# The convolution half of a fused block: from an order written out by hand to tasks of the list scheduler

## The chip, the cores and the metric

The kernel runs on one core of one Trainium2 chip. The metric is the device time of one execution in microseconds (us). A core has five engines with an instruction stream each: PE (matrix multiply, with PEld for its weight loads), DVE (vector), ACT (scalar activation), POOL and SP. Each engine executes its stream in program order and waits on semaphores where an operand is not there yet. In this kernel SP issues nearly all DMA transfers, so SP's order is the order in which transfers are asked for.

## The reference, cut to what matters

```python
def _A_ref(q, k, v, shift_k, ssm_k, ssm_D):       # S = 2048, D = 512, ks = 4
    k_shift = sum(k_pad[:, t:t + S, :] * shift_k[:, ks - 1 - t] for t in range(ks))
    kv = k_shift * v
    y = irfft(rfft(kv, 2 * S) * rfft(ssm_k, 2 * S))[:S]     # causal convolution along S
    y = y + kv * ssm_D
    return q * y
def _B_ref(x, w1, w2, w3, w4):                    # F = 1792
    h = gelu(layernorm(x) @ w1)
    x1 = x + shifted_by_channel_quarter(h) @ w2
    return x1 + gelu(layernorm(x1) @ w3) @ w4
h = x + _A_ref(layernorm(x), A_k, A_v, ...)       # x = A_q
out = h + _B_ref(layernorm(h), ...)
```

Inputs and output are bf16 of shape (1, 2048, 512); sums are in float32.

## The kernel before, in words

The kernel has two halves. The **first half** (lines 218 to 499) computes the convolution `_A_ref` with a Fourier transform of length 4096 in two steps, both as matmuls. The **second half** (lines 501 to 770) does the inverse's last step, the gate with q, and all of `_B_ref`.

The first half goes through these stages; the names are those of the functions and of the tiles in the profile.

- **Loads.** SP issues the filter `A_ssm_k` in 4 pieces into `ra` (L229), k in 4 transposing transfers into `rb` (L232), v in 2 into `rb` (L236). q comes later (L374).
- **Tables.** DVE and ACT compute sines for the transform (`trig`, L321 to L330, table `ftab` in `rf`) from angles that DVE forms at L315 and L318.
- **Transposed filter** (L356 to L361). PE turns the filter in 8 blocks of 8 transposes, ACT empties five of them and DVE three. L364 adds the D row.
- **First step of the filter** (`step1`, L348, 16 times): 8 matmuls into a double bank `ps`, 128x1024 float32, that DVE or ACT evicts into `rc`. After each 4 of them an **exchange** (L353) of 4 transfers moves the result across partitions into `rd`, 16 in all.
- **Shift and product** (`shift`, L406 and L409, 16 times): 16 matmuls with diagonal weights make the four-tap shift of k, DVE multiplies by v into `xk`.
- **First step of k*v** (`step1` again, 16 times, into `ra`) and its exchange into `rc` (L353).
- **Second step of the filter** (`spectrum`, L396, tile `psg`, 16 times): 4 matmuls, evicted into `rd`.
- **Transposed tables** (`tables`, 4 times) and the inverse's table (`backs`).
- **Statistics of q** (`qstat`, L414 and L415, 16 times, on DVE), closed by `qnorm` on POOL.
- **The loop of products** (L493 to L496, 16 turns): `fwd` does the second step of k*v (`psk`), ACT spreads it to `asb` (L339), DVE makes two products with the filter's spectrum (`pr`, L473 and L474); two turns later `inv` does 8 matmuls (L484) into `psv` or `psva`, evicted into `vst`, and SP sends it across partitions into `ra` (L488).

The order of all that is the order of the Python code. One loop (from L433 on) puts a shift, a first step of k*v, a spectrum and a statistic of q behind each other in every turn; the rest of the spectra and the tables follow it, and the loop of products comes last. `evac` (L335) sends an eviction to ACT or DVE by a running count of their costs. PSUM has three double banks (`ps_a`) for most stages and two single ones (`ps_c`) for shifts, transposes and tables; the loop of products gives those two to `psv`. `xk` has 8 buffers, `asb`, `pr` and `vst` have tiles of their own.

The second half is ordered by the class `Plan` (L35). Each task has a cost for each engine that may do it, a list of tasks that it depends on, and rings of buffers that it takes and drops. `forward` is a list scheduler that gives each free engine the ready task of highest priority; `solve` repeats it 40 times with other priorities and keeps the shortest plan; `emit` writes the instructions in that order. The costs set only the order: on the chip every engine runs its stream as soon as its operands are there. The second half's first task is `inv1` (L549), then the gate (`z`, L560, on ACT).

Of the kernel before, what the change touches and what calls it, by code (L numbers as in the profile page):

```python
# [34 lines left out]
class Plan:  # L35
# [6 lines left out]

    LAT = 0.2

    def __init__(self, pools, rounds=40):
        self.pools, self.rounds, self.t = pools, rounds, []

    def add(self, opts, fn, deps=(), take=None, many=1, drop=None, part=0, rank=0.0, name=None):
        n = len(self.t)
        deps = {d["n"] for d in deps if d is not None}  # L50
        if drop is not None:
# [3 lines left out]
                 users=[0] * many, rank=rank, name=name)  # L55
# [5 lines left out]
    def forward(self, prio):  # L61
        ts = self.t
        done, eng, free, order = {}, {}, {e: 0.0 for t in ts for e in t["opts"]}, []
# [4 lines left out]
        while ready:  # L68
            best = None
            for n in ready:  # L70
# [7 lines left out]
                at0 = {e: max([at0, free[e]] + [done[d] + (0.0 if eng[d] == e else self.LAT) for d in t["deps"]]) for e in t["opts"]}  # L78
# [12 lines left out]
            if t["drop"] is not None:  # L91
                m, i = t["drop"]
                users[m][i] -= 1
                if not users[m][i]:
                    gone[m, i] = done[n]
# [6 lines left out]
        return max(done.values()), order, done, eng  # L102

    def backward(self, done, eng):
# [4 lines left out]
        while ready:  # L109
            best = None  # L110
            for n in ready:
                e = eng[n]
                at = max([free[e]] + [left[o] + (0.0 if eng[o] == e else self.LAT) for o in ts[n]["out"]])
# [12 lines left out]
    def solve(self):  # L126
        tail, best, rnd = {}, None, random.Random(1)
        for t in reversed(self.t):
            tail[t["n"]] = t["rank"] + min(t["opts"].values()) + max((tail[o] + self.LAT for o in t["out"]), default=0.0)
# [18 lines left out]
def kernel(  # L148
# [69 lines left out]
    ps_a = p0.enter_context(tc.tile_pool(name="ps_a", bufs=3, space=PSUM))  # L218
    p1 = ExitStack()
    ps_c = p1.enter_context(tc.tile_pool(name="ps_c", bufs=2, space=PSUM))  # L220
    xkp = p1.enter_context(tc.tile_pool(name="xkp", bufs=8))
# [6 lines left out]
    for c in range(DC):  # L228
        nc.sync.dma_start(hnat[:, c, :], A_ssm_k[c * P:(c + 1) * P, :])  # L229
    k_r = A_k.rearrange("o n d -> (o n) d")  # L230
    for c in range(DC):
        nc.sync.dma_start_transpose(kT[:, c, 16:KW], k_r[:, c * P:(c + 1) * P])  # L232
    v_r = A_v.rearrange("o (p b) d -> p (o b) d", p=P)
    q_r = A_q.rearrange("o (p b) d -> p (o b) d", p=P)
    for g in range(2):
        nc.sync.dma_start(v_sb[:, 8 * g:8 * g + 8, :], v_r[:, 8 * g:8 * g + 8, :])  # L236
# [27 lines left out]
    for i in range(10):  # L264
        pt = ps_c.tile([P, D], F32, name="ptw", tag="pk")
        nc.tensor.matmul(pt[:], lhsT=wup[:, 0:P], rhs=wup[:], start=True, stop=True)
# [47 lines left out]
    for r in range(2):  # L314
        nc.vector.tensor_tensor(out=uu[:, :, r, :, :],  # L315
                                in0=a1[:].rearrange("p (k t) -> p k t", t=2).unsqueeze(3).to_broadcast([P, NH, 2, 32]),
                                in1=b2[:, r, :].unsqueeze(1).unsqueeze(1).to_broadcast([P, NH, 2, 32]), op=ADD)
    nc.vector.tensor_scalar(out=ui, in0=ui, scalar1=4095, scalar2=None, op0=OP.bitwise_and)  # L318

    def trig():  # L320
        nc.scalar.activation(fall[:, :, 0:32], uall, ACT.Sin, bias=negpi[:], scale=SC)  # L321
        nc.vector.tensor_scalar(out=fall[:, :, 32:64], in0=fall[:, :, 0:32], scalar1=sgo[:], scalar2=None, op0=MUL)
        nc.gpsimd.tensor_scalar(out=ftab[:, 0, :, 0, 0:32], in0=s0[:, :, 0, :], scalar1=lo_, scalar2=1.0, op0=MUL, op1=MUL)
# [8 lines left out]
    load = {"A": 0.0, "V": 0.0}  # L332

    def evac(o, i, n, fast=False, eng=None):
        ca, cv = 0.05 + 0.833e-3 * n, 0.065 + (0.52e-3 if fast else 1.042e-3) * n  # L335
        e = eng or ("A" if load["A"] + ca <= load["V"] + cv else "V")
        if e == "A":
            load["A"] += ca
# [28 lines left out]
    for bl in range(NL):  # L367
# [3 lines left out]
        if bl == 1:  # L371
            trig()
# [59 lines left out]
    for b in range(NB):  # L432
# [11 lines left out]
        if b >= 4:  # L444
            qstat(b - 4)
# [351 lines left out]
```

## Time and profile before

| | |
|---|---|
| median of 3 runs | 265.88 us (265.42 to 269.07) |
| the profiled execution's own time | 268.6 us |
| its span, first to last instruction | 266.8 us |
| mean granted clock of PE | 0.953 |
| busy: PE, DVE, ACT, POOL | 231.9, 161.9, 143.3, 54.1 us |
| moved by DMA | 28.08 MB |

The times are those of whole executions; the profile is one execution, 1.8 us of which lie outside the span. Its time is 2.7 us above the median. In a row of a group, the last number before the second bar is the mean duration in ns, and what follows it is how long the engine stood idle just before, and who ended that. A row of the chain of waits has start, length, engine, tile and line. PE's busy time counts matmuls that overlap, so a busy PE is not yet a full one.

### The profile page before, as it was taken

How to read it: one execution, taken by the hardware profiler on the slowest of the kernel's cores; microseconds unless marked ns; L12 is line 12 of the kernel's file. 1: busy time of each engine (PE TensorE's matmuls, PEld its weight loads, DVE VectorE, ACT ScalarE, POOL GpSimd, SP SyncE). 2: the span in 40 equal slices, each digit the busy share in tenths (PEclk: the TensorE clock that was granted, in tenths of full speed). 3: DMA queues.
4: the chain of work that ended last, by engine and by line, in shares of the span. 5: the costliest groups of instructions: out<-in, count | busy, mean ns of one | idle time of the engine just before them, and what ended most of it. 6: DMA issues, size and time to landing. Idle time of an engine off the chain costs nothing.

```text
span 266.8 us, 4530 instructions
## 1 busy us (share of the span) xinstructions
PE 231.9 (87%) x1803; PEld 119.0 (45%) x1803; DVE 161.9 (61%) x323; ACT 143.3 (54%) x202; POOL 54.1 (20%) x101
## 2 busy tenths in 40 slices
PE   8665957999579988665988999999999999999994
PEld 3522834555242222224655756445444444444441
DVE  7986807669927998299999994898022250013322
ACT  3638152788479998266867856556500046632000
POOL 3503000000130102029998442251000000000000
PEclk9999995999959999796899999999999999999999
DMA  7999990340701465891000000000011110000111
GB/s 241 249 271 360 407 346 37 142 160 15 295 11 41 153 241 179 295 396 39 1 2 0 4 0 0 2 1 0 2 39 39 39 39 2 0 20 20 42 39 39
DMA packets 18791, 28.08 MB, mean 105 GB/s; under 512 B 10065, under 2 KB 13906, under 8 KB 17234
## 3 DMA queue, kind: packets, MB, share of 16 engines
q1 hardware_dynamic: 17952, 26.74, 29.0%
q0 software_dynamic: 288, 1.05, 1.3%
q8 instruction: 14, 0.23, 0.4%
q10 hardware_dynamic: 530, 0.01, 0.1%
q14 instruction: 7, 0.06, 0.1%
HBM read 11.02 MB, written 2.10 MB: 49 GB/s over the span
## 4 chain that ended last, share of the span: by engine, by line
PE 57%; DVE 24%; DMA 6%; ACT 5%; POOL 4%; issue 2%; ACTq 0%; POOLq 0%
PE mm L717 18%; PE mm L702 18%; DVE st L566 4%; PE pk L406 4%; PE mm L662 3%; DVE rd L571 3%; DMA q_sb<-in_A_q_dram 3%; DMA rd<-rc 2%; DVE rt L315 2%; PE psg L396 2%; DVE vst L342 2%; ACT rc L339 2%; PE psk L396 2%; PE psva L484 2%; DVE pr L474 1%
## 5 line engine op out<-in xcount | busy, mean ns | idle before, releaser
L708 ACT ACTIVATE ra<-mm 128x512 bf16<-128x512 f32 x56 | 33.4, 597 | 49.7 <-PE mm L702 49.6
L702 PE MATMUL mm<-rc,rb 128*128 128x512 bf16 x224 | 50.8, 379 | 0.0
L717 PE MATMUL mm<-rt,ra 128*128 128x512 bf16 x224 | 49.0, 379 | 0.0
L725 DVE TENSOR_TENSOR ob<-mm,rd 128x512 bf16<-128x512 f32 x16 | 11.1, 692 | 61.4 <-PE mm L717 61.4
L717 PEld LDWEIGHTS <-ra 128*128 128x128 bf16 x224 | 22.0, 98 | 26.4
L702 PEld LDWEIGHTS <-rb 128*128 128x128 bf16 x224 | 21.6, 98 | 24.8
L406 PE MATMUL pk<-diag,rb 128*128 128x128 bf16 x256 | 19.8, 238 | 4.4 <-DVE xk L409 4.3
L406 PEld LDWEIGHTS <-rb 128*128 128x128 bf16 x256 | 18.3, 150 | 8.8 <-issue 7.5
L637 PE MATMUL mm<-rc,rf 128*128 128x256 bf16 x128 | 17.8, 295 | 0.0
L530 ACT COPY rc<-ptx 128x512 bf16<-128x512 bf16 x26 | 14.6, 583 | 4.6 <-PE ptx L623 4.6
L662 PE MATMUL mm<-rf,rb 128*128 128x512 bf16 x64 | 16.2, 380 | 1.0 <-ACT rb L643 0.9
L339 ACT CAST asb<-psk 128x1024 bf16<-128x1024 f32 x16 | 16.1, 1030 | 0.5 <-ACT asb L339 0.4
L571 DVE SCALAR_TENSOR_TENSOR rd<-q_sb,qmv,z 128x512 bf16<-128x512 bf16 x16 | 12.7, 792 | 4.6 <-ACT z L560 4.6
L414 DVE BATCH_NORM_STATS2 qst<-q_sb 128x6 f32<-128x512 bf16 x16 | 10.9, 680 | 6.5 <-DMA q_sb<-in_A_q_dram 6.5
L409 DVE TENSOR_TENSOR xk<-pk,rb 128x512 bf16<-128x512 f32 x16 | 10.9, 681 | 6.3 <-PE pk L406 6.2
L560 ACT ACTIVATE z<-mm,qrs 128x512 f32<-128x512 f32 x16 | 10.6, 697 | 7.4 <-PE mm L549 5.7
L637 PEld LDWEIGHTS <-rf 128*128 128x128 bf16 x128 | 13.2, 106 | 2.3
L667 DVE SCALAR_TENSOR_TENSOR q_sb<-rd,cr,mm 128x512 bf16<-128x512 bf16 x16 | 11.7, 733 | 3.7 <-PE mm L662 3.7
L396 PE MATMUL psg<-rd,rf 128*64 128x512 bf16 x64 | 10.3, 418 | 4.2 <-ACT rd L339 4.0
L396 PEld LDWEIGHTS <-rf 128*64 128x64 bf16 x128 | 5.7, 115 | 17.2 <-issue 16.2
L473 DVE TENSOR_TENSOR pr<-asb,rd 128x1024 bf16<-128x1024 bf16 x16 | 11.0, 687 | 3.5 <-ACT asb L339 3.5
L339 ACT CAST rd<-psg 128x1024 bf16<-128x1024 f32 x13 | 13.0, 1028 | 0.0
(224 smaller groups left out, 347.2 us busy)
## 6 DMA issues: line engine op xcount, KB each, us to landing
rd<-rc SPq DMA_DIRECT2D x16, 256.0 KB, 6.0
rc<-ra SPq DMA_DIRECT2D x16, 256.0 KB, 2.4
ra<-vst SPq DMA_DIRECT2D x16, 256.0 KB, 2.4
ra<-in_A_ssm_k_dram SPq DMA_DIRECT2D x4, 512.0 KB, 5.1
rb<-in_A_v_dram SPq DMA_DIRECT2D x2, 1024.0 KB, 8.0
q_sb<-in_A_q_dram SPq DMA_DIRECT2D x2, 1024.0 KB, 8.3
out_dram<-ob SPq DMA_DIRECT2D x16, 128.0 KB, 1.8
rb<-in_B_w_dram SPq DMA_DIRECT2D x1, 1792.0 KB, 7.3
```

Source lines behind the costliest of these rows:

```text
L339: nc.scalar.copy(o, i)
L396: nc.tensor.matmul(ps[64 * t:64 * t + 64, r, :], lhsT=ftab[:, kh, r, t, :], rhs=z[:, kh, t, :], start=True, stop=True)
L406: nc.tensor.matmul(pk[:, c * P:(c + 1) * P], lhsT=kT[:, c, 16 + b - j:KW - 16 + b - j + 1:16], rhs=diag[:, c, j, :], start=(j == 0), stop= ...
L530: nc.scalar.copy(o, i)
L571: nc.vector.scalar_tensor_tensor(out=h_sb[:, b, :], in0=q_sb[:, b, :], scalar=qmv[:, b, 0:1], in1=tl["z", b][:], op0=SUB, op1=MUL)
L637: nc.tensor.matmul(pw_[:, j * 256:(j + 1) * 256], lhsT=w1_sb[:, k, m * P:(m + 1) * P], rhs=hnT[:, k, p * 256:(p + 1) * 256], start=(k == 0 ...
L662: nc.tensor.matmul(px[:], lhsT=shifted(m, b), rhs=w2_sb[:, m, :], start=(m == 0), stop=(m == DC - 1))
L667: nc.vector.scalar_tensor_tensor(out=x1[:, b, :], in0=hbm[:, b, :], scalar=tl["cr", b // 2][:, b % 2:b % 2 + 1], in1=tl["x", b][:], op0=MU ...
L702: nc.tensor.matmul(pg[:], lhsT=w3_sb[:, k, fc * P:(fc + 1) * P], rhs=lnT[:, k, g * 512:(g + 1) * 512], start=(k == 0), stop=(k == DC - 1))
L708: nc.scalar.activation(gbuf[:, g % 2, fc, :], tl["g", g, fc][:], ACT.Gelu_apprx_tanh)
L717: nc.tensor.matmul(po[:], lhsT=gbuf[:, g % 2, fc, i * P:(i + 1) * P], rhs=w4_sb[:, fc, :], start=(fc == 0), stop=(fc == FC - 1))
L725: nc.vector.tensor_tensor(out=ob[:], in0=tl["o", 4 * g + i][:], in1=xh1[:, b, :], op=ADD)
```

## The change

The first half's stages become tasks of a `Plan` too. What that does:

- **DMA as an engine "D".** Each load and each exchange is a task with a cost on D and a landing latency `lat` of 1.75 us that its users wait for in the plan. D is SP's queue. The order of the loads becomes filter, k, then q, v, q, v in halves; the exchanges come behind all four.
- **One PSUM ring.** `ps_a` has 4 double banks, taken by every stage in turn; `ps_c` and `ps_v` are gone. Shifts are done in pairs, so that a product of k and v is 128x1024, once for two blocks. `xk` has 4 buffers of four blocks' width.
- **Product buffers in dead memory.** `asb` (3), `pr` (4) and `vst` (5 buffers) lie in `rb`, where k and v were. The first spread depends on the last shift and the last product with v.
- **Order.** The scheduler interleaves. Of the filter's 16 first steps four come behind the first shifts, 11 of its 16 spectra come into the loop of products, the inverse's table near its end. Table copies go whole to one engine, here DVE.

The arithmetic stays, and the number of transfers. The second half's plan has the same tasks, and its rows stand in the same order on all five engines.

Three places in the order. **SP from its first load**, `ra` being the filter's place, `rb` that of k and v, `rd<-rc` the filter's exchange and `rc<-ra` that of k*v. Before:

```order
L229 DMA ra<-in_A_ssm_k_dram 128x2048 x4
L232 DMA_TRANSPOSE rb<-in_A_k_dram 128x2048 x4
L236 DMA rb<-in_A_v_dram 128x4096 x2
L353 DMA rd<-rc 32x4096 x16
L374 DMA q_sb<-in_A_q_dram 128x4096 x2
L353 DMA rc<-ra 32x4096 x16
L488 DMA ra<-vst 32x4x1024 x16
```

And of the change:

```order
L329 DMA ra<-in_A_ssm_k_dram 128x2048 x4
L329 DMA_TRANSPOSE rb<-in_A_k_dram 128x2048 x4
L329 DMA q_sb<-in_A_q_dram 128x4096
L329 DMA rb<-in_A_v_dram 128x4096
L329 DMA q_sb<-in_A_q_dram 128x4096
L329 DMA rb<-in_A_v_dram 128x4096
L401 DMA rd<-rc 32x4096 x16
L401 DMA rc<-ra 32x4096 x16
L546 DMA ra<-rb 32x4x1024 x16
```

q has moved ahead of the filter's exchange, its first half ahead of v.

**DVE around the first product of spectra** (`pr` before, `rb<-rb,rd` in the change; `rt` are the tables, `rd<-psg` and `rd<-pg` spectra of the filter, `qst` and `qmv` a statistic of q). Before:

```order
L383 TENSOR_SCALAR rt<-pt 128x512
L390 TENSOR_SCALAR rt<-pt 128x128
L342 CAST rd<-psg 128x1024
L383 TENSOR_SCALAR rt<-pt 128x512
L342 COPY rt<-pt 128x512
L473 TENSOR_TENSOR pr<-asb,rd 128x1024
L474 TENSOR_TENSOR pr<-asb,rd 128x1024
```

And of the change:

```order
L474 TENSOR_SCALAR rt<-tb 128x512
L323 CAST rd<-pg 128x1024
L500 BN_STATS qst<-q_sb 128x6
L501 BN_AGGR qmv<-qst 128x2
L323 CAST rd<-pg 128x1024
L531 TENSOR_TENSOR rb<-rb,rd 128x1024
L532 TENSOR_TENSOR rb<-rb,rd 128x1024
```

The products stand where two of DVE's spectra are done; before, all of them were.

**ACT from the last first step of k*v into the loop** (`ra<-pc` that step, `asb<-psk` before and `rb<-pw` now the spread, `vst` before and `rb<-pv` now the inverse). Before:

```order
L339 CAST ra<-ps_1055 128x1024
L339 COPY rt<-pt 128x512 x2
L339 CAST rd<-psg 128x1024 x3
L339 CAST f_71<-ptf 128x512 x2
L339 COPY rt<-pt 128x512
L339 CAST asb<-psk 128x1024 x3
L339 CAST vst<-psva 128x1024
L339 CAST asb<-psk 128x1024
```

And of the change:

```order
L321 CAST ra<-pc 128x1024 x7
L321 CAST rd<-pg 128x1024 x3
L321 CAST rb<-pw 128x1024 x3
L321 CAST rd<-pg 128x1024 x2
L321 CAST rb<-pw 128x1024
L321 CAST rb<-pv 128x1024 x2
L321 CAST rb<-pw 128x1024
L321 CAST rb<-pv 128x1024
```

Spectra stand between spreads and inverses now, and no table copy is left on ACT here.

The diff, cut to its core:

```diff
-    ps_a = p0.enter_context(tc.tile_pool(name="ps_a", bufs=3, space=PSUM))
-    p1 = ExitStack()
-    ps_c = p1.enter_context(tc.tile_pool(name="ps_c", bufs=2, space=PSUM))
-    xkp = p1.enter_context(tc.tile_pool(name="xkp", bufs=8))
+    ps_a = p0.enter_context(tc.tile_pool(name="ps_a", bufs=4, space=PSUM))
+    xkp = p0.enter_context(tc.tile_pool(name="xkp", bufs=4))
...
+    plan = Plan({"big": 4, "xk": 4, "asb": 3, "pr": 4, "vst": 5}, 40, {"V": 5.6, "A": 6.2, "G": 2.8, "PE": 5.5, "D": 1.8})
...
+    EV = {"A": 1.04, "V": 1.2}
+    LAND = 1.75
...
+    for g in range(2):
+        task(("v", g), {"D": 3.0}, load(v_sb[:, 8 * g:8 * g + 8, :], v_r[:, 8 * g:8 * g + 8, :]), lat=LAND)
+    for g in range(2):
+        task(("q", g), {"D": 3.0}, load(q_sb[:, 8 * g:8 * g + 8, :], q_r[:, 8 * g:8 * g + 8, :]), lat=LAND)
...
+    task(("uu",), {"V": 2.4}, angles)
...
+    for bl in range(NL):
+        for h in range(4):
+            task(("F", bl, h), {"PE": 0.56}, step1(("ph", bl, h), lambda bq, bl=bl: xh[:, 4 * bl + bq, :], h),
+                 [("TE", c, bl // 2) for c in range(DC)] + [("dr",)], take="big")
+            task(("FE", bl, h), EV, out1(("ph", bl, h), zch, bl, h), drop=("F", bl, h))
+        task(("FX", bl), {"D": 2.6}, exchange(zh, zch, bl, range(4)), [("FE", bl, h) for h in range(4)], lat=LAND)
...
+    for p in range(NB // 2):
+        task(("S", p), {"PE": 2.3}, shift(p), [("k", c) for c in range(DC)] + [("diag",)] + ([("S", p - 1)] if p else []), take="big")
+        task(("X", p), {"V": 1.25}, gated(p), [("v", p // 4)] + ([("X", p - 1)] if p % 2 else []), take=None if p % 2 else "xk",
+             drop=("S", p))
+    for bl in range(NL):
+        for h in range(4):
+            task(("K", bl, h), {"PE": 0.56}, step1(("pc", bl, h), lambda bq, bl=bl: tl["xk", bl][:, bq, :], h),
+                 [("X", 2 * bl + 1)], take="big", drop=("X", 2 * bl))
+            task(("KE", bl, h), EV, out1(("pc", bl, h), zck, bl, h),
+                 [("F", 3, 3)] if bl > 1 else [("T", c, 1) for c in range(DC)], drop=("K", bl, h))
+        for kl in range(4):
+            task(("KX", bl, kl), {"D": 0.66}, exchange(zk, zck, bl, [kl]), [("KE", bl, h) for h in range(4)] + [("FX", 3)], lat=LAND)
...
+    for kb in range(4):
+        task(("B", kb), {"PE": 0.6}, tables(kb), [("tg",)], take="big")
+        task(("BE", kb), {"A": 1.7, "V": 1.1}, tabled(kb), drop=("B", kb))
...
+    for b in range(NB):
+        task(("qs", b), {"V": 0.85}, qstat(b), [("q", b // 8)])
+    task(("qn",), {"G": 3.3}, qnorm, [("qs", b) for b in range(NB)])
+    for kh in range(NH):
+        task(("G", kh), {"PE": 0.56}, step2(("pg", kh), zh, kh), [("FX", bl) for bl in range(NL)] + [("tg",)], take="big")
+        task(("GE", kh), EV, lambda e, kh=kh: copy(e, gst[:, kh, :, :], tl["pg", kh][:]), drop=("G", kh))
+
+    asb = [view(rb, 1024 * i, 1024, "p (r d) -> p r d", r=2) for i in range(3)]
+    prb = [view(rb, 3072 + 2048 * i, 2048, "p (m r d) -> p m r d", m=2, r=2) for i in range(4)]
+    vsb = [view(rb, 11264 + 1024 * i, 1024, "p (t d) -> p t d", t=2) for i in range(5)]
...
+    for kh in range(NH):
+        task(("W", kh), {"PE": 0.56}, step2(("pw", kh), zk, kh), [("KX", bl, kh // 4) for bl in range(NL)] + [("BE", kb) for kb in range(4)] + [("be",)] +
+             ([("V", kh - 3)] if kh > 2 else []), take="big")
+        task(("A", kh), {"A": 1.04}, spread(kh), [("S", NB // 2 - 1), ("X", NB // 2 - 1)], take="asb", drop=("W", kh))
+        task(("P", kh), {"V": 1.38}, products(kh), [("GE", kh)], take="pr", drop=("A", kh))
+        task(("V", kh), {"PE": 1.0}, inverse(kh), [("BE", kh // 4), ("be",)], take="big", drop=("P", kh))
+        task(("VE", kh), EV, lambda e, kh=kh: copy(e, ring("vst", vsb, ("vst", kh)), tl["pv", kh][:]), take="vst", drop=("V", kh))
+        task(("VX", kh), {"D": 0.66}, back(kh), [("KX", NL - 1, 3)], drop=("VE", kh), lat=LAND)
+    plan.emit()
```

336 lines of the change are left out of this document (161 added, 175 removed).

## The prediction

> **What bounds the kernel now.** I read the stretches first: one row for each stage, with busy time of PE, PEld, DVE, ACT and POOL, granted clock, DMA share and GB/s.
>
> ```profile
> 0.00:26.50 26.50, 17.40 (x186) 9.37 (x187) 21.33 (x45) 14.19 (x16) 8.26 (x28) 1.00 0.99 278
> 26.50:40.00 13.50, 10.72 (x156) 8.20 (x156) 5.73 (x7) 5.45 (x6) 0.08 (x1) 1.00 0.96 381
> 40.00:79.60 39.60, 33.10 (x381) 19.22 (x382) 27.55 (x54) 26.61 (x32) 3.15 (x2) 0.85 0.28 111
> 79.60:109.10 29.50, 25.10 (x191) 7.61 (x188) 25.47 (x37) 26.86 (x30) 2.44 (x4) 0.96 0.47 166
> 109.10:266.80 157.70, 145.62 (x896) 74.58 (x896) 81.80 (x181) 70.19 (x120) 40.16 (x67) 0.97 0.12 40
> ```
>
> The last row is the second half, which the change leaves alone. In the four rows of the first half DVE is busy 80.1 of 109.1 us, ACT 73.1, PE 86.3 (the third row's mean clock of 0.85 is a full clock with stretches at half, below). No engine is full there except in the fourth row, where ACT and DVE both stand near 90%. So the first half is bound by order: who waits for whom, and each stage waits for the one ahead. The chain of waits says where:
>
> ```profile
> 26.56 6.07 DMA rd<-rc
> 32.65 7.34 DMA q_sb<-in_A_q_dram
> 40.01 0.70 DVE qst L414
> 41.55 1.86 PE pk L406 x16
> ...
> 73.94 2.75 ACT rd L339 x3
> ...
> 80.65 0.70 DVE pr L473
> ```
>
> The reader is to see two seams. From 26.6 to 40.0 the chain is DMA: q is issued on SP behind the 16 exchange transfers, and DVE, in program order, stands at the statistics of q with the k*v products behind it. From 72 to 80 the loop of products has not begun, because the last spectra and tables are still being emptied. The list of waits gives these seams their prices:
>
> ```profile
> DVE qst L414 <- DMA q_sb<-in_A_q_dram: 6.5, 1, 6.5
> PE pk L406 <- DVE xk L409: 4.3, 1, 4.3
> PE psg L396 <- ACT rd L339: 4.0, 1, 4.0
> ```
>
> **The change, part by part.** Landmarks of the timeline (start, length), then lengths of work that follows work without a gap, from the chain:
>
> ```profile
> 27.59 5.18 PE L406 MATMUL pk<-diag,rb 128*128 128x128 bf16 x80
> 79.60 2.85 ACT L339 CAST asb<-psk 128x1024 bf16<-128x1024 f32 x3
> 107.45 1.23 DVE L342 CAST vst<-psv 128x1024 bf16<-128x1024 f32 x1 [0.70 <-PE psv L484]
> 112.54 2.42 ACT L560 ACTIVATE z<-mm,qrs 128x512 f32<-128x512 f32 x4 [4.85 <-PE mm L549]
> ```
>
> ```profile
> 14.02 0.41 DVE ra L364
> 14.48 0.64 PE ps_281 L348 x8
> 15.14 2.37 DVE rc L342 x2
> ...
> 70.14 0.59 DVE qst L414
> 70.93 0.59 DVE qst L414
> ...
> 78.62 0.42 DVE rt L342
> ...
> 84.13 0.55 PE psk L396 x4
> 84.68 0.97 PE psva L484 x8
> ...
> 95.88 0.60 DVE pr L474
> ```
>
> That gives: a 128x1024 eviction of PSUM 1.19 us on DVE (2.37 over 2) and 0.92 on ACT (2.75 over 3); a statistic of q 0.79; a 128x512 copy of a table 0.42; a pair of products 1.20; a second step 0.55 and an inverse 0.97 on PE; 32 shift matmuls 2.07 (5.18 over 80, times 32).
>
> *Start to 22 us.* DVE now empties four of the eight transposed blocks instead of three and flips the table's signs ahead of its phase evictions. Both were there before, later or on ACT:
>
> ```profile
> L342 DVE COPY ra<-pt 128x1024 bf16<-128x1024 bf16 x3 | 2.0, 685 | 0.1
> L322 DVE TENSOR_SCALAR rf<-rf,sgo 128x2048 bf16<-128x2048 bf16 x1 | 0.8, 754 | 2.6 <-ACT rf L321 2.6
> ```
>
> So the first step of the filter can start 0.7 us later than at 14.48, and DVE begins its evictions at 14.43 + 0.69 + 0.75 = 15.9. Five take 5.9, to 21.8; ACT takes seven at 0.92. Twelve of 16 steps are then done and PE is free for the shifts at about 22.5, where before it began them at 27.59.
>
> *Loads.* SP now issues q, v, q, v in halves behind the transposes of k, and the exchanges come after.
>
> ```profile
> L236 SPq DMA_DIRECT2D rb<-in_A_v_dram x2: 420/523/626, 15.6 to 16.2; - x2
> DMA to landing us min/median/max: 6.4/8.0/9.5
> ```
>
> The halves of v landed at about 15.6 + 6.4 = 22.0 and 16.2 + 9.5 = 25.7, that is 3.7 us apart. The first places in the queue are now q's: I estimate q at 22.0, v at 25.7, q at 29.4, v at 33.1. DVE's four first statistics run from 22.0 to 25.2 and the first product of k and v at 25.7, so the 6.5 us wait for q is gone. What is late next is the second half of v. The fifth product wants it, and its shift is ready at 22.5 + 5 x 2.07 = 32.9, so PE covers it; without that cover each us of a later v is a us of the end. Seven shifts keep PE until 22.5 + 7 x 2.07 = 37.0, and DVE's seventh product ends at 38.2. The product over 1024 columns has no row before; two rows of half its size would be 1.36 (681 ns each alone), an eviction of that size 1.19; I take 1.19, as DVE is fed from PSUM in both, and 0.17 x 8 = 1.4 us goes to the range.
>
> *From 38.2 to the first spectral product.* DVE's order lists: 7 statistics (5.5), the last product of k and v (1.2), 5 evictions of first steps (6.0), 12 table copies (5.0) with a small one (0.2), 2 spectra (2.4). Sum 20.3, so 58.5. PE, ACT and the four double banks are looser there: PE has 19 first steps, one pair of shifts, tables and five spectra, some 18 us, and ACT 14 evictions, 13 us. On SP the filter's fourth exchange now waits for the last of these evictions of ACT's, at about 45, and behind it in that queue stand all 16 transfers of k*v. They need 0.6 us each on SP and 2.4 to land:
>
> ```profile
> L353 SPq DMA_DIRECT2D rc<-ra x16: 459/593/601, 45.5 to 71.7; - x16
> rc<-ra SPq DMA_DIRECT2D x16, 256.0 KB, 2.4
> ```
>
> The first group of them is ready at about 46, so little waits there, and the spectra start after 52. The last eviction for k*v comes at about 52.5 on this count; four transfers and the landing make 57, ahead of the first product. I add 1.0 us for handoffs through one ring: 59.5, against 80.65 before. These 21 us are not all gain, since 11 of 16 spectra, before finished by then, now run inside the loop.
>
> *The loop.* ACT, from about 58.5: 16 spreads, 12 inverses, 6 spectra, the inverse table = 35 at 0.92, 32.2 us. DVE: 16 x 1.20 + 9 x 1.19 = 29.9. PE: 16 x 0.55 + 16 x 0.97 + 11 x 0.55 + 1.0 = 31.4. All three are nearly even. Before, the loop from the first spread (79.60) to the last eviction's end (107.45 + 1.23 = 108.68) took 29.1 for ACT's 27 evictions, 24.8, a fill of 0.85. With no gap the new loop is 32.2, with that fill 37.9. I take 37.2 (the spectra are independent work that fills gaps, so a fill of 0.87), and its end is 95.7.
>
> *Hand-over.* The first gate came 112.54 - 108.68 = 3.9 us after the last eviction. This stays: last store, landing, first inverse matmuls. w1 and w2 wait for the tables' region and now start earlier; w3 is issued behind the last store as before. The product buffers in the k, v region wait for the last shift and product, 20 us before their first use. Nothing is priced there.
>
> *Sum.* 108.7 - 95.7 = 13.0 us. The profiled execution took 268.6 us, span 266.8; it becomes 255.6, span 253.8. The median of the runs, 265.88, lies 2.7 below that execution; from there it is **252.9 us**.
>
> **A rule against it.** First the rows: clock granted in stretches of 2 us, and one first step (8 matmuls) at each clock.
>
> ```profile
> 22.00:24.00 2.00, 0.21 (x4) 0.00 (x0) 0.52 (x1) 2.00 (x2) 0.00 (x0) 1.00 0.84 279
> ...
> 42.00:44.00 2.00, 2.00 (x22) 1.30 (x19) 1.93 (x6) 0.00 (x0) 0.00 (x0) 0.50 0.04 8
> ...
> 43.34 1.04 PE L348 MATMUL ps_663<-xk,f_70 128*32 128x512 bf16 x8
> ...
> 47.16 0.61 PE L348 MATMUL ps_704<-xk,f_70 128*32 128x512 bf16 x8
> ```
>
> A PE idle of about 2 us (22 to 24) kept the full clock; the 4.3 us ahead of 41.55 (in the list of waits) were followed by half clock, with the same step at 1.04 instead of 0.61. The Trainium skill, "TensorE: Matmul & The Clock Gate", section "A second HAM failure mode: psum-queue depth-cycling", says that a PE which cycles through PSUM and idles briefly between groups can swing between half and full clock. The loop before, which also cycles a ring, stood at 0.96 in the stretch above, so this trace does not bear the rule out for short waits; the change makes such waits more frequent, and it stays as a rival below.
>
> **The rivals.** *Half clock (slower).* From the first spectrum on PE waits at every slot of the one ring, the gate closes and stays closed. Then 31.4 us of PE work becomes 31.4 x 1.04 / 0.61 = 53.5, PE is the bound, and five spectra and the last tables ahead (about 5 us) add 3.5: the end is 58.5 + 3.5 + 53.5 = 115.5, 6.8 us behind the 108.7 of before: 272.7 us. For it: waits everywhere, three even engines. Against: 0.96 in the old loop and 1.00 through the gap at 22. It decides from about 27 of the 31.4 us at half clock (0.70 us lost for each; the gain is gone at a loop of 50.2 us).
>
> *Late v and late last exchange.* The filter's fourth exchange now waits for first steps that sit behind the products in the ring. If the exchanges that are already issued slow the second half of v from 33 to 40 (q, issued behind exchanges, needed 7.3 us), the chain moves some 4.5 us, and a loop that starts with a worse fill (0.80, 40.3 us) loses 3 more: gain 5.5, 260.4 us. For it: DMA share 0.96 to 0.99 up to 40 us. Against: PE's shifts hide the first 1.6 us or more, and the issue order puts v ahead.
>
> *No gaps.* If the spectra fill every gap, the loop takes 32.2 and the handoffs nothing: 95.7 falls to 58.5 - 1.0 + 32.2 = 89.7, a gain of 19.0 and 246.9 us. Against: each eviction hands a slot back to an in-order PE.
>
> **How the numbers follow.** Forecast 0.64, late exchange 0.18, no gaps 0.11, half clock 0.07. The likeliest gives 252.9. The low end, 247.5, lies at the no-gaps case; the high end, 262, takes in the late exchange with the 1.4 us of wider products on top; half clock stays out, and so does half of the no-gaps case. A measurement of this kernel tells about 2% from no change, that is below 260.6 or above 271.2: faster is 0.64 + 0.11 and a third of the late exchange, 0.06, together 0.81; within 2% 0.12; slower 0.07.
>
> **What would show it.** DVE's statistics of q start near 22 without a wait for q; PE's shifts start at 22 to 24 and not at 27.6; the first spectral product stands at 58 to 61; DVE and ACT are over 85% busy from there to 96; the last eviction of the first half ends at 94 to 97, the first gate 4 us later; the second half takes as long as before; granted clock in the loop is at 0.95 or more. The prediction is wrong if the wait for q is replaced by one for v of several us, if PE stands at 0.5 in the loop, or if the loop is longer than 40 us.

## The result, and the profile after

| | before | after |
|---|---|---|
| median of 4 runs each | 267.48 us (265.42 to 270.42) | 253.63 us (252.35 to 255.81) |
| the profiled execution | 268.6 us | 253.12 us |
| its span | 266.8 us | 251.4 us |
| mean granted clock of PE | 0.953 | 0.965 |
| first product of spectra starts | 80.65 | 59.08 |
| first gate starts | 112.54 | 97.12 |

The ratio of the times is 0.9515, with a 95% interval of 0.9393 to 0.9638; it goes by the means and leaves out one slow run of the kernel before, 270.42 us. The span shrank by 15.4 us, and the first gate of the second half comes 15.4 us earlier: all of the gain is made in the first half, and none is given back behind it.

First the stretches of the changed kernel, cut at its own landmarks: start of the shifts, first product, end of the last eviction, first gate. The columns are those of the prediction's first fence.

```profile
0.00:22.50 22.50, 17.05 (x171) 9.45 (x172) 19.14 (x43) 13.35 (x15) 8.36 (x28) 0.85 0.99 266
22.50:59.10 36.60, 33.26 (x489) 24.29 (x487) 34.06 (x62) 19.44 (x22) 2.06 (x2) 1.00 0.70 279
59.10:92.60 33.50, 28.77 (x254) 10.54 (x251) 29.95 (x41) 31.53 (x34) 3.52 (x5) 1.00 0.45 158
...
97.10:251.40 154.30, 142.40 (x864) 73.38 (x861) 81.77 (x181) 70.26 (x120) 40.17 (x67) 0.98 0.11 38
```

And the second half of the kernel before, cut from its own first gate:

```profile
112.50:266.80 154.30, 142.22 (x864) 73.34 (x861) 81.80 (x181) 70.19 (x120) 40.16 (x67) 0.97 0.10 36
```

The second half lasts 154.3 us in both. In the first half the picture has turned round: between 22.5 and 59.1 DVE is busy for 34.06 of 36.6 us (93%), where before it had 5.73 of 13.5 and 27.55 of 39.6. From 59.1 on ACT is busy for 31.53 of 33.5 (94%) and DVE for 29.95. What was bound by order is now nearly bound by an engine, DVE first and then ACT. The granted clock is 1.00 from 22.5 to 92.6, where 0.85 stood in the long stretch before.

The list of waits (engine and tile that wait, who ends the wait, total us, times, longest us), up to 115 us:

```profile
ACT rc L321 <- PE ph L392: 14.9, 5, 11.5
...
PE pt L381 <- DVE ra L323: 3.3, 1, 3.3
...
DVE rc L323 <- PE ph L392: 1.5, 2, 1.0
```

The waits of 6.5, 4.3 and 4.0 us that carried the prediction are gone, and no wait for a load of q or v has taken their place. ACT's 14.9 us are slack: it is busy for 19.44 of the 36.6 us in which DVE is full. Two waits are new. PE stands 3.3 us at the start, for a copy that DVE makes behind the angles, and the first spread waits 1.3 us for an exchange of k*v. The timeline shows the latter and the rest of the landmarks, DVE's and ACT's first:

```profile
5.58 5.76 DVE L342 TENSOR_TENSOR rt<-a_161,b_163 128x1024 int16<-128x1024 int16 x2
...
11.26 0.68 DVE L323 COPY ra<-pt 128x1024 bf16<-128x1024 bf16 x1
...
18.30 4.79 DVE L323 CAST rc<-ph 128x1024 bf16<-128x1024 f32 x4 [0.48 <-PE ph L392]
...
23.00 0.68 DVE L500 BATCH_NORM_STATS2 qst<-q_sb 128x6 f32<-128x512 bf16 x1
...
38.07 1.19 DVE L432 TENSOR_TENSOR xk<-pk,rb 128x1024 bf16<-128x1024 f32 x1
...
59.08 0.69 DVE L531 TENSOR_TENSOR rb<-rb,rd 128x1024 bf16<-128x1024 bf16 x1 [1.09 <-ACT rb L321]
```

```profile
58.03 2.84 ACT L321 CAST rb<-pw 128x1024 bf16<-128x1024 f32 x3 [1.20 <-PE pw L454]
...
91.52 1.09 ACT L321 CAST rb<-pv 128x1024 bf16<-128x1024 f32 x1
...
97.12 2.42 ACT L609 ACTIVATE z<-mm,qrs 128x512 f32<-128x512 f32 x4 [3.00 <-PE mm L598]
```

Then PE's:

```profile
11.99 1.86 PE L381 MATMUL pt<-ident,ra 128*128 128x128 bf16 x16 [3.29 <-DVE ra L323]
14.64 7.87 PE L392 MATMUL ph<-ra,f_70 128*32 128x512 bf16 x96 [0.78 <-DVE ra L323]
22.45 12.16 PE L424 MATMUL pk<-diag,rb 128*128 128x128 bf16 x192
...
57.37 1.49 PE L454 MATMUL pw<-rc,rf 128*64 128x512 bf16 x12 [1.33 <-DMA rc<-ra]
```

And the chain of waits, from the filter's first steps to the fourth product of k and v, and across the seam into the loop:

```profile
14.64 3.63 PE ph L392 x32
18.30 3.56 DVE rc L323 x3
...
22.51 8.12 PE pk L424 x128
30.66 1.23 DVE xk L432
...
54.39 2.85 DMA rc<-ra
...
57.37 0.64 PE pw L454 x4
58.03 1.02 ACT rb L321
59.08 0.69 DVE rb L531
```

DVE's last four evictions of the filter end at 18.30 + 4.79 = 23.09, its statistics of q follow at once, its seventh product ends at 39.26, and the loop runs from the first spread, 58.03, to 91.52 + 1.09 = 92.61. The first gate comes 4.5 us later.

### The profile page after: what moved, and what is told of

It reads as the page before. It is cut to its first block, busy times and chain, and to the rows that moved or that the text cites. A ratio compares the mean times of both kernels' runs of the same rounds, so it can differ in the third digit from the quotient of the medians.

```text
span 251.4 us, 4538 instructions
## 1 busy us (share of the span) xinstructions
PE 225.0 (90%) x1803; PEld 118.7 (47%) x1803; DVE 164.9 (66%) x325; ACT 136.1 (54%) x191; POOL 54.1 (22%) x101
## 4 chain that ended last, share of the span: by engine, by line
PE 55%; DVE 29%; ACT 5%; POOL 4%; DMA 2%; issue 2%; SPq 1%; ACTq 0%; POOLq 0%
PE mm L766 19%; PE mm L751 19%; DVE st L615 4%; PE mm L711 3%; DVE rd L620 3%; PE pk L424 3%; DVE qst L500 2%; DVE xk L432 2%; DVE rt L342 2%; ACT rb L321 2%; DVE rb L531 2%; DVE rb L532 2%; ACT ra L321 2%; DVE rd L323 2%; PE ph L392 2%
## 5 line engine op out<-in xcount | busy, mean ns | idle before, releaser
L751 PEld LDWEIGHTS <-rb 128*128 128x128 bf16 x224 | 21.6, 98 | 24.8
L321 ACT CAST rc<-ph 128x1024 bf16<-128x1024 f32 x11 | 10.8, 1025 | 14.9 <-PE ph L392 14.9
L541 PE MATMUL pv<-rb,rt 64*128 64x512 bf16 x128 | 16.6, 378 | 2.0 <-DVE rd L323 1.3
L321 ACT CAST rb<-pw 128x1024 bf16<-128x1024 f32 x16 | 16.2, 1027 | 1.9 <-PE pw L454 1.2
L424 PEld LDWEIGHTS <-rb 128*128 128x128 bf16 x256 | 16.3, 148 | 1.5 <-issue 1.5
L424 PE MATMUL pk<-diag,rb 128*128 128x128 bf16 x256 | 16.6, 226 | 0.3 <-ACT ra L321 0.3
L598 PE MATMUL mm<-ra,f_71 32*128 32x512 bf16 x128 | 10.2, 426 | 3.6 <-ACT z L609 1.5
L640 POOL TENSOR_TENSOR rr<-uw,mhalf 128x4 f32<-128x4 f32 x8 | 10.4, 1295 | 11.4 <-DVE hm L629 11.4
L321 ACT CAST rb<-pv 128x1024 bf16<-128x1024 f32 x12 | 12.1, 1039 | 1.3 <-PE pv L541 1.3
L454 PEld LDWEIGHTS <-rf 128*64 128x64 bf16 x128 | 6.6, 108 | 12.8 <-issue 9.2
```

Of the source, the lines that this page charges most:

```text
L321: nc.scalar.copy(o, i)
L424: nc.tensor.matmul(pk[:, i, c * P:(c + 1) * P], lhsT=kT[:, c, 16 + b - j:KW - 16 + b - j + 1:16], rhs=diag[:, c, j, :], start=(j == 0), st ...
L541: nc.tensor.matmul(ps[:, t, :], lhsT=tt[hs, min(x, 2), kh, :], rhs=pr[hs, x // 2, x % 2, :], start=(x == 0), stop=(x == 3))
L751: nc.tensor.matmul(pg[:], lhsT=w3_sb[:, k, fc * P:(fc + 1) * P], rhs=lnT[:, k, g * 512:(g + 1) * 512], start=(k == 0), stop=(k == DC - 1))
```

## The experiments

The change has five parts at least: an early q, one ring of four slots, spectra inside the loop, buffers in dead memory, and a search that sets the order. **The theory** was the prediction's: the gain is seams that close, q's the largest single one, and the loop holds its pace on a full clock. **The rivals**: early q is nearly all of it; the four slots are; the search is, whatever the parts; or the plan's costs, which differ from the measured ones, cap the gain. The table gives each run's median, its ratio to the kernel before on the same chip, and two landmarks of its profile, which the clock of the second half does not touch. A landmark comes from one execution; between the change and the runs made from it, medians and first gates differ by the same amount to within 1.3 us. The kernel before had medians of 267.04 to 268.57 us beside them.

| run | median, us | ratio (95%) | first product | first gate |
|---|---|---|---|---|
| before | 267.48 | 1 | 80.65 | 112.54 |
| after | 253.63 | 0.9515 (0.9393 to 0.9638) | 59.08 | 97.12 |
| e1, early q alone | 264.22 | 0.9907 (0.9859 to 0.9955) | 76.44 | 108.27 |
| e2, late q | 254.03 | 0.9526 (0.9422 to 0.9630) | 61.31 | 98.09 |
| e3, spectra first | 255.24 | 0.9588 (0.9513 to 0.9663) | 67.75 | 98.75 |
| e4, ring split 3 and 1 | 255.58 | 0.9613 (0.9519 to 0.9708) | 67.53 | 98.97 |
| e5, fewer buffers | 251.46 | 0.9455 (0.9378 to 0.9532) | 59.44 | 95.19 |
| e6, measured costs | 249.13 | 0.9360 (0.9272 to 0.9447) | 57.22 | 92.92 |
| e7, ring of 3 | 260.22 | 0.9765 (0.9656 to 0.9873) | 64.20 | 104.94 |
| e8, one round of search | 262.14 | 0.9842 (0.9752 to 0.9933) | 66.16 | 105.78 |
| e9, only the angles' cost | 256.25 | 0.9589 (0.9511 to 0.9666) | 63.16 | 100.43 |
| e10, another seed | 251.58 | 0.9408 (0.9348 to 0.9467) | 59.22 | 95.05 |
| e11, measured costs, 400 rounds | 249.62 | 0.9347 (0.9291 to 0.9403) | 58.07 | 93.35 |
| e12, measured costs, another seed | 248.67 | 0.9295 (0.9228 to 0.9361) | 58.15 | 93.14 |

### e1: the kernel before, with q's loads ahead of the exchanges

```diff
     for g in range(2):
+        nc.sync.dma_start(q_sb[:, 8 * g:8 * g + 8, :], q_r[:, 8 * g:8 * g + 8, :])
         nc.sync.dma_start(v_sb[:, 8 * g:8 * g + 8, :], v_r[:, 8 * g:8 * g + 8, :])
...
-    for g in range(2):
-        nc.sync.dma_start(q_sb[:, 8 * g:8 * g + 8, :], q_r[:, 8 * g:8 * g + 8, :])
```

> The hand-ordered kernel with only SP's loads changed: q, v, q, v in halves ahead of the filter's exchange. Landmark is the start of the first gate on ACT: 112.5 us before, 97.1 with the whole change. Theory (the gain is the order of all stages, and q's wait is one seam of several): DVE's 6.5 us wait for q and the half clock behind it go, the other seams stay; first gate at 105 to 107, gain 5.5 to 7 us, ratio to before 0.975 to 0.98. Rival (the early q is all of it): first gate at 97 to 99, gain 13 us or more. Second rival (q is hidden behind the next wait anyway, for v or for the filter's exchange): gain under 2 us.

The wait for q is gone, but the first gate comes only 4.3 us earlier, 28% of the change's 15.4. The chain of this run from the shifts on shows why it is not 6.5:

```profile
28.44 5.60 PE pk L405 x80
34.04 0.54 PE ps L349 x8
34.59 1.15 PE pk L405 x16
```

With q there, PE runs shifts and first steps back to back and sets the pace; DVE waits for it at 13 products of k and v, 7.4 us in all (6.2 at 9 before). Of PE's own loss, its 4.3 us stall is gone, and the half clock behind it too, as 40 to 60 us show, the kernel before first and then e1:

```profile
40.00:60.00 20.00, 18.45 (x206) 11.10 (x206) 13.32 (x28) 13.04 (x15) 0.00 (x0) 0.83 0.28 113
```

```profile
40.00:60.00 20.00, 19.90 (x261) 12.40 (x258) 13.82 (x28) 16.72 (x20) 0.00 (x0) 1.00 0.27 108
```

Some is paid back: the shifts begin 0.8 us later (28.44, before 27.59), a half clock has come up at 26 to 30 (below), and PE stands 1.0 us at its first spectrum. These sizes were not isolated one from another; their balance is 4.3 us. The later seams stay in this run's list of waits:

```profile
DVE xk L408 <- PE pk L405: 7.4, 13, 1.8
...
PE psg L395 <- ACT rd L340: 4.0, 1, 4.0
...
DVE rd L343 <- PE psg L395: 3.7, 3, 2.8
```

So early q alone is refuted as the whole, and the theory's size for it, a gate at 105 to 107, was too large.

### e2: the change, with q's loads behind the filter's exchanges in the dependencies

```diff
-        task(("q", g), {"D": 3.0}, load(q_sb[:, 8 * g:8 * g + 8, :], q_r[:, 8 * g:8 * g + 8, :]), lat=LAND)
...
+        task(("q", g), {"D": 3.0}, load(q_sb[:, 8 * g:8 * g + 8, :], q_r[:, 8 * g:8 * g + 8, :]), [("FX", NL - 1)], lat=LAND)
```

> The changed kernel with q's loads behind the filter's fourth exchange in the plan, as they stood behind it before the change. The planner is free to put the statistics of q elsewhere. Theory (the order counts, q's early issue is one way of several): the statistics, 12.6 us of DVE, move behind about 50 us and into the loop, where DVE has 3 to 4 us of room; first gate at 98 to 106, loss 1 to 9 us. Rival (the early q is all of the gain): first gate at 108 us or later. Second rival (nothing hangs on q once the order is planned): within 1 us of 97.1.

The edit does less than was meant. The loads of q depend on the filter's fourth exchange group, and the planner did that group first: SP issues it, then the loads of v and q, and only then the other three groups.

```profile
19.34 2.47 SPq L399 DMA_DIRECT2D rd<-rc  x4
...
22.49 0.44 SPq L329 DMA_DIRECT2D q_sb<-in_A_q_dram  x1
...
24.37 21.45 SPq L399 DMA_DIRECT2D rd<-rc  x12
```

q is issued some 6 us later than in the change (16.04), and 10 us earlier than before (32.65). The gate is 1.0 us later, and in place of the wait for q there is one for v:

```profile
DVE xk L432 <- DMA rb<-in_A_v_dram: 4.0, 1, 4.0
```

A q that is 6 us late costs little once the rest can be moved around it. What a q at its old place, behind all 16 transfers, would cost a planned order was not measured.

### e3: every spectrum of the filter ahead of the loop again

```diff
-             ([("V", kh - 3)] if kh > 2 else []), take="big")
+             ([("V", kh - 3)] if kh > 2 else []) + [("GE", j) for j in range(NH)], take="big")
```

> The changed kernel with one more dependency: the second steps of k*v wait in the plan for all 16 spectra of the filter, so that none of them stands in the loop of products. Theory (the spectra in the loop fill its gaps and start it earlier): the loop starts about 6 us later (11 spectra, shared by ACT and DVE), lasts about 29 us as before instead of 34.6, and gets a worse fill; first gate at 98.5 to 101, loss 1.5 to 4 us against the change. Rival (interleaving the spectra is the main gain): loss of 8 us or more. Second rival (it is neutral, the work is only moved): within 1 us.

The first product comes 8.7 us later, and the gate 1.6 us. The loop has shrunk by what was put ahead of it: spectra inside the loop mostly move work. The 1.6 us lie in the 1.5 to 4 that were expected.

### e4 and e5: a ring split in 3 and 1, and fewer product buffers

```diff
-    ps_a = p0.enter_context(tc.tile_pool(name="ps_a", bufs=4, space=PSUM))
+    ps_a = p0.enter_context(tc.tile_pool(name="ps_a", bufs=3, space=PSUM))
+    ps_s = p0.enter_context(tc.tile_pool(name="ps_s", bufs=1, space=PSUM))
...
-            task(("T", c, g), {"PE": 0.6}, turn(c, g), [("h", c)], take="big")
+            task(("T", c, g), {"PE": 0.6}, turn(c, g), [("h", c)], take="sml")
```

In e4 the transposes, the shifts and the tables take that one double bank of their own, and the rest take the three.

> The changed kernel with PSUM split again: a ring of three double banks for the steps, spectra and inverses, and one double bank for transposes, shifts, tables and the inverse's table. The planner orders anew for it. Theory (one ring is a means, the order is what counts): the pairs of shifts alternate with their product on one bank (2.0 + 1.2 us a pair, 8 pairs, 26 us instead of 17), so the first half loses 3 to 8 us; most of the gain stays. Rival (the ring of four is the gain): back at 108 us or later for the first gate. Second rival: no loss.

```diff
-    plan = Plan({"big": 4, "xk": 4, "asb": 3, "pr": 4, "vst": 5}, 40, ...
+    plan = Plan({"big": 4, "xk": 4, "asb": 3, "pr": 3, "vst": 4}, 40, ...
```

> The changed kernel with as many product buffers as before: asb 3, pr 3, vst 4 instead of 3, 4, 5. Theory (buffers in the dead k, v region are enabling room, not speed): first gate within 1 us of 97.1. Rival (the longer rings let DVE and ACT run ahead): a loop 3 us longer or more, first gate at 100 or later.

The split ring ends 1.9 us later, less than the 3 to 8 expected, the fewer buffers 1.9 us earlier, outside the 1 us expected. A smaller resource cannot help a kernel by itself; that e5 gains says that each of these runs is also another plan, found by a search. How much that alone does is measured by e10.

### e10 and e9: the scatter of the search

```diff
-        tail, best, rnd = {}, None, random.Random(1)
+        tail, best, rnd = {}, None, random.Random(self.seed)
...
+    plan = Plan({"big": 4, "xk": 4, "asb": 3, "pr": 4, "vst": 5}, 40, ..., seed=2)
```

> The changed kernel with another seed of the planner's random search, nothing else. It says how far two plans of the same tasks and costs lie apart, and so how much of a difference between planned kernels may be luck. Theory (the luck is about 2 us, as the kernel with fewer buffers, a tighter problem, came out 1.9 us ahead): first gate within 2 us of 97.1. Rival: more than 3 us away, and then no experiment that plans anew tells less than that.

Another seed, and nothing else, moves the first gate by 2.1 us.

```diff
-    task(("uu",), {"V": 2.4}, angles)
+    task(("uu",), {"V": 5.7}, angles)
```

> The changed kernel with one cost of the planner set to what its row shows: 5.7 us instead of 2.4 for the angle table; all other costs as in the change. In the changed kernel this table ends 3.3 us after the plan, a copy of the transposed filter stands behind it on DVE, and PE waits 3.3 us for the slot, after which it runs at half clock. Theory (this one cost makes most of the 4.2 us by which the kernel with all costs measured is ahead): first gate at 93 to 95. Rival (the other costs, or luck of the search): within 1.5 us of 97.1.

By the theory the corrected cost alone should have won; it lost 3.3 us of the gate. But 5.7 us is not the angles' own length. In this run they take 2.35 us for two instructions, and it is the next one on DVE that is long, 3.98 us where it took 0.68 in the change:

```profile
5.57 2.35 DVE L342 TENSOR_TENSOR rt<-a,b 128x1024 int16<-128x1024 int16 x2
7.96 3.98 DVE L347 TENSOR_SCALAR rt<-rt 128x2048 int16<-128x2048 int16 x1
```

Beside the long instruction stands a product on POOL each time, the diagonal weights `diag`. First this run, then the change:

```profile
7.73 3.67 POOL L366 TENSOR_TENSOR diag<-ident,ssk_bf 128x2048 bf16<-128x2048 bf16 x1 [4.96 <-DMA ssk_bf<-in_A_shift_k_dram]
```

```profile
6.20 4.06 POOL L366 TENSOR_TENSOR diag<-ident,ssk_bf 128x2048 bf16<-128x2048 bf16 x1 [3.42 <-DMA ssk_bf<-in_A_shift_k_dram]
```

In the change it starts ahead of the second angle instruction (6.71), which then takes 4.63 us; the first took 1.22. Here its operand lands later, and the instruction that DVE starts behind it, at 7.96, is the long one. All fourteen traces fit this: twelve are as the change, e7 is as this run. So the DVE instruction that starts beside this product takes some 3.3 us longer, which no cost in the plan knows, and the plan's 2.4 us for the angles was about right. The theory that this one wrong cost was what held the change back falls, and with it its premise. What made this plan the worse one was not isolated. As far as these two replanned runs tell, 2 to 3 us either way may be the search's. e2, e3, e4 and e5 all lie inside that. A loss of 1.6 or 1.9 us with such a scatter on it leaves room for some 5 us; how much each of those parts carries they do not show.

### e7: the same ring with three slots

```diff
-    plan = Plan({"big": 4, "xk": 4, "asb": 3, "pr": 4, "vst": 5}, 40, ...
+    plan = Plan({"big": 3, "xk": 4, "asb": 3, "pr": 4, "vst": 5}, 40, ...
```

The pool has three double banks as well, and the fourth pair of banks stays unused.

> The changed kernel with a ring of three double banks instead of four (one bank pair unused), planned anew. Theory (PE, ACT and DVE are nearly even in the loop, so a slot less makes them wait for each other): loop 2 to 5 us longer than 34.6, first gate at 99 to 104. Rival (four are more than enough): within 1 us of 97.1. Second rival (slots set the pace): 106 or later.

The gate is 7.8 us later, well outside the scatter and more than expected: 5.1 us by the first product, 2.7 in and behind the loop. Ahead of the loop DVE waits 4.0 us for the filter's first steps (1.5 in the change). In the loop ACT waits for PE, DVE for ACT, and PE for DVE's eviction of a spectrum, which holds the slot that an inverse is to have:

```profile
ACT rb L321 <- PE pv L541: 3.2, 7, 1.4
...
DVE rb L531 <- ACT rb L321: 3.0, 2, 2.7
...
PE pv L541 <- DVE rd L323: 1.9, 2, 1.3
```

Of the parts that were taken away one by one, the fourth slot is the dearest but for the search (e8). Before, PSUM had the same eight banks, cut into three pairs and two singles that only some stages could use. e4, with three pairs and one more of its own, lost 1.9: the number of slots counts, and that all stages share them does not show.

### e8: one round of the search

```diff
-    plan = Plan({"big": 4, "xk": 4, "asb": 3, "pr": 4, "vst": 5}, 40, ...
+    plan = Plan({"big": 4, "xk": 4, "asb": 3, "pr": 4, "vst": 5}, 1, ...
```

> The changed kernel with one round of the planner instead of 40: the first list schedule with priorities by the longest path to the end, no search. Theory (the tasks and engines as such bring the order, the search trims): first gate at 98 to 102. Rival (the search is what finds it): 105 or later. Second rival: no difference, within 1 us of 97.1.

The first list schedule has all the parts of the change, and wins 112.54 - 105.78 = 6.8 us. The other 8.7, more than half of the 15.4, come with the search's 39 further rounds. So the gate stands where the rival had put it, at 105 or later, and not at the 98 to 102 of the theory: tasks and engines alone bring less than half of the gain. It is not the wait for q that comes back; this run's list has none for q or v. Both halves of the first half gain: the first product moves from 66.16 to 59.08, and what follows it from 39.6 us to 38.0.

### e6, e11 and e12: the planner's costs as measured

```diff
-    EV = {"A": 1.04, "V": 1.2}
-    LAND = 1.75
+    EV = {"A": 0.92, "V": 1.14}
+    LAND = 2.4
...
-    task(("uu",), {"V": 2.4}, angles)
+    task(("uu",), {"V": 5.7}, angles)
...
-        task(("S", p), {"PE": 2.3}, shift(p), ...
+        task(("S", p), {"PE": 2.03}, shift(p), ...
...
-        task(("P", kh), {"V": 1.38}, products(kh), [("GE", kh)], take="pr", drop=("A", kh))
+        task(("P", kh), {"V": 1.2}, products(kh), [("GE", kh)], take="pr", drop=("A", kh))
```

Twenty numbers in all are set to durations that the profiles of the two kernels show.

> The changed kernel with the planner's costs set to durations that the profiles show (angles 5.7 us instead of 2.4, evictions 0.92 on ACT and 1.14 on DVE, products 1.2, shifts 2.03, transposed loads 3.3 each, landing 2.4). Theory (the plan's order is near its limit; DVE has some 80 us of work that starts at 5.6 us): first gate between 94 and 98. Rival (the mis-sized angles, which block the ring and PE for 3.3 us at the start, cost several us): first gate at 93 or earlier. Second rival (accurate costs make the plan brittle, since handoffs are no longer covered by the padding): first gate at 99 or later.

```profile
0.00:22.50 22.50, 17.21 (x210) 9.73 (x211) 20.03 (x43) 17.51 (x20) 8.10 (x28) 1.00 0.98 256
...
57.20:88.20 31.00, 28.83 (x256) 10.63 (x255) 29.95 (x42) 30.46 (x34) 4.52 (x5) 1.00 0.44 150
```

The gate comes 4.2 us before that of the change. It stands where the rival put it, at 93 or earlier, but not by the rival's reason, the angles, whose cost alone lost (e9). The loop stretch is 31.0 us with ACT busy for 30.46 (98%): this is the case that the prediction called "no gaps". ACT has also done more before 22.5 us, 17.51 against 13.35.

e11 has the same costs and 400 rounds, e12 the same costs and the other seed:

```diff
-    plan = Plan({"big": 4, "xk": 4, "asb": 3, "pr": 4, "vst": 5}, 40, ...
+    plan = Plan({"big": 4, "xk": 4, "asb": 3, "pr": 4, "vst": 5}, 400, ...
```

> Measured costs and 400 rounds of search instead of 40. Theory (with true costs a better plan on paper is a better one on the chip): first gate at 91 to 93, no later than the 92.9 of 40 rounds. Rival (the plan is at its limit, DVE's work being some 80 us from 5.6 us on): within 0.5 us of 92.9. Second rival (the longer search fits the model's errors): 94 or later.

> Measured costs with the other seed. Theory (the 4.2 us of the measured costs are more than luck): first gate at 95 or earlier, and at least 2 us ahead of the same seed with the costs of the change. Rival (luck): 96 or later.

The three gates with measured costs lie within 0.4 us (92.92 to 93.35), those with the change's costs at 97.12 and 95.05: 1.9 us at the same second seed, just short of the 2 expected, and 4.2 at the first. The direction is the same at both seeds. Ten times the rounds brought nothing at this seed. e12, e11 and e6, with ratios of 0.9295 to 0.9360, are the best of all kernels measured here; their intervals overlap. All three lie below the change's 0.9515, and e12's whole interval lies below that of the change (0.9393 and up).

## Why the prediction was right, point by point

The forecast, 252.9 us, met a median of 253.63. The mechanism held, but so close an agreement is luck, since two errors cancel. The profiled execution was put at 255.6 us and took 253.12: the gain in the span is 15.4 us where 13.0 was forecast. And the median was put 2.7 us below that execution, as it lay before; it came 0.5 above. The base was 265.88 us from three runs, where the four runs beside the change give 267.48.

- **The seams.** "The 6.5 us wait for q is gone" held: the statistics start at 23.00, forecast 22.0. PE's shifts start at 22.45 (22.5). No wait for v came. In their place DVE is 93% busy, and ACT then 94%. But the price of a seam is not the longest wait in it: 4.3 us for q alone (e1), since PE sets the pace as soon as q is early.
- **The start.** The filter's evictions on DVE were forecast from 15.9 to 21.8 and ended at 23.09. PE stood 3.29 us behind the angles of 5.76 us, since a slot of the ring was held by a transposed block that DVE empties behind them, at 11.26. The plan has 2.4 us for the angles, what they take when POOL's product does not run beside them (e9); the 5.76 us stood in the profile before too, and the prediction did not set them against the plan. Behind that stall PE ran first steps at half clock (last section), and DVE waited 1.5 us for them. The seventh product ended 1.1 us late (39.26, forecast 38.2), but not for that: the shifts began on time, and the chain goes through them to the fourth product at 30.66. From there DVE has four products and five statistics without a gap, where the prediction let PE's shifts set the pace up to the seventh.
- **From there to the first product**: 19.8 us, forecast 20.3 and 1.0 for handoffs. The one gap on DVE is 1.09 us, close to the 1.0. DVE's work was 18.7 us, less than counted, most of the difference in the table copies: 4.1 us with the small one, from 50.74 to 54.84, where 5.2 were counted. The first product stood at 59.08, forecast 59.5. The landing of the last exchange, forecast at 57 and so hidden, came at 57.24: with 1.3 us of PE's time behind it, a small form of the rival "late last exchange".
- **The loop** is the mis-sized term: 34.6 us from 58.03 to 92.61, forecast 37.2. ACT's 35 evictions, 32.2 us of work, are as counted; the fill, that work as a share of the stretch, is 0.93, not 0.87. What was misread is the old loop. Its 29.1 us, from which the prediction took a fill of 0.85, run to DVE's last eviction at 108.68. ACT's own last one ended 2.5 us earlier:

```profile
105.16 1.01 ACT L339 CAST vst<-psva 128x1024 bf16<-128x1024 f32 x1
```

From its first spread at 79.60 to 106.17, ACT's 24.8 us of work filled 26.6: 0.93 before as well. In the change ACT has the last eviction itself, so no such tail stands behind it. With 0.93 the forecast would have been some 34.5 us. That "the spectra are independent work that fills gaps" is not needed for the number, and not shown: in e3, with no spectrum in the loop, ACT's 28 evictions filled 29.2 us to 0.88, which speaks for it, but that is one other plan.
- **The hand-over** took 4.5 us, forecast 3.9. "This stays" missed by 0.6.
- **The sum**: 0.47 us for the first spread (58.03, forecast 58.5), 2.62 in the loop, minus 0.65 at the hand-over, is 2.44 on top of 13.0, and that makes the 15.4.
- **The rival of half clock** did not come: 1.00 is granted from 22.5 to 92.6 in a loop that hands one ring of four slots round three even engines. The rule that the prediction set against the change, from the Trainium skill, "TensorE: Matmul & The Clock Gate", section "A second HAM failure mode: psum-queue depth-cycling", finds no case in this loop. One part of the gain has no price in the prediction: before, a mean clock of 0.85 over 39.6 us means some 5.9 us of full clock not granted, an estimate, behind the very waits that the change removes. The prediction counted the new stages with rows at full clock and so took it in unnamed. How much of it is in the gain was not isolated; the first of those half-clock stretches went with the stall for q in e1, and is part of its 4.3 us.

What stays open is the worth of the spectra in the loop, of sharing the ring and of the buffers apart. They lie inside the scatter of the search. And since 8.7 of the 15.4 us are gone with one round of it, the gain belongs to the order that was found more than to any one part.

## What to carry to other kernels

Price a wait by the engine that sets the pace once it is gone: DVE's 6.5 us were worth 4.3. Where a planner sets the order, put the profile's durations into its costs as a set, since the angles' cost alone lost 3.3 us of the first gate and all together won 4.2 at one seed and 1.9 at another, and run a second seed before a difference of 2 to 3 us is given to a part. Ask of a long duration whether it is the instruction's own or comes from what runs beside it, as with the angles. Let the planner search: here 39 more rounds were worth 8.7 us. And look for one more slot in a ring that every stage passes through; here the fourth was worth 7.8 us. Before a fill is carried over to a new loop, see which engine ends the old one.

## What the runs showed of the hardware that was not expected

The same idle of PE did not have the same effect on its clock. In the kernel before, and in e1, PE stands 2.19 us ahead of the same first step at 24.4:

```profile
24.40 0.62 PE L348 MATMUL ps_409<-ra,f_70 128*32 128x512 bf16 x8 [2.19 <-ACT rc L339]
```

```profile
24.39 0.61 PE L349 MATMUL ps<-ra,f 128*32 128x512 bf16 x8 [2.19 <-ACT rc L340]
```

Then the stretches of 2 us, of the kernel before and of e1:

```profile
22.00:24.00 2.00, 0.21 (x4) 0.00 (x0) 0.52 (x1) 2.00 (x2) 0.00 (x0) 1.00 0.84 279
...
26.00:28.00 2.00, 1.81 (x30) 0.80 (x23) 1.93 (x3) 1.78 (x2) 0.58 (x3) 1.00 1.01 422
```

```profile
22.00:24.00 2.00, 0.21 (x4) 0.00 (x0) 0.53 (x1) 2.00 (x2) 0.00 (x0) 1.00 0.99 418
...
26.00:28.00 2.00, 1.86 (x24) 0.57 (x16) 1.66 (x2) 1.35 (x2) 0.56 (x3) 0.54 0.97 291
```

The clock of e1 fell to 0.54 and that of the kernel before did not, after equal work and equal idle. Each is one execution, and the mean clock of the kernel before itself ranged from 0.940 to 0.968 over its runs, so this may be chance of the execution and not of the kernel. In e6 an idle of 2.41 us ahead of a first step at 12.91 kept 1.00. So the idle of about 2 us that "kept the full clock", which the prediction read from one row, is no bound. The Trainium skill, "TensorE: Matmul & The Clock Gate", section "What's actually happening", has activity counted in windows of about 3.4 us that run freely, and the clock halved after an idle window of that length. A window that runs freely would let the same idle end in two ways, which agrees with these two rows; that 2.19 us were enough in e1 does not agree with an idle window of 3.4, and there the measurement decides. In the changed kernel the idle of 3.29 us ahead of 11.99 was followed by half clock as well:

```profile
12.00:14.00 2.00, 1.86 (x16) 1.61 (x15) 1.84 (x4) 1.42 (x1) 0.00 (x0) 0.50 1.17 163
...
16.00:18.00 2.00, 2.00 (x24) 0.68 (x20) 1.23 (x1) 1.31 (x2) 1.84 (x7) 0.50 1.29 252
```

What it cost was not isolated. Four first steps took 3.63 us from 14.64, where one took 0.64 in the kernel before, DVE waited 1.5 us for them, and the chain goes through both to the shifts, which still began when they were forecast, at 22.45. e6, granted 1.00 in its first 22.5 us, began them at 23.16, but behind work in another order.

The other is the DVE instruction beside POOL's product `diag`: 4.63 us where the same instruction took 1.22 (the change), and 3.98 us where it took 0.68 (e9).
